# A new start for a gated SSM + GELU kernel: first tokens in 128-row pieces, weight strips on two hardware queues, third GELU stage moved up

## The chip, the cores and the metric

The kernel runs on one core of a Trainium2 chip. The metric is the device time of one execution in microseconds (us). A run of a single core has no second die beside it to compare with, so a run counts as fast unless it is more than 1.5% above the fastest run of the same kernel; only fast runs are compared. Each run also has a granted clock: the share of TensorE's full clock that the chip's throttle let through. The kernel before takes 217.74 us (median of three, 217.73 to 218.23).

## The reference

For 2048 tokens of width 640, a gate mixes a diagonal state-space model (SSM) with a GELU block:

```python
x = A_x                                                   # 1 x 2048 x 640, bfloat16
g = sigmoid((x * gate_w).sum(-1, keepdims=True))
# A: dt = exp(log_dt); Lam_bar = exp(dt * Lambda); B_bar = ((Lam_bar - 1) / Lambda)[:, None] * B
#    h_t = Lam_bar * h_(t-1) + x_t B_bar^T   (complex, 640 states, serial over the tokens)
#    a   = 2 * real(h C^T) + x * Dskip
# B: b   = gelu(x @ w1 + b1) @ w2 + b2      (640 -> 1728 -> 640)
return g * a + (1 - g) * b
```

## The kernel before

Tokens are processed in four chunks of 512. All products need the tokens turned, 128 features on the partitions (`xT`). TensorE (PE) then has four kinds of stage: `ff1` (the product with w1, GELU stage), `ssm` (the products with B), `fin_b` (the product with w2) and `fin_a` (the product with C). VectorE (DVE) makes the scan of the SSM, ScalarE (ACT) the evictions, which copy results out of a bank (the memory that PE writes). `colA` and `colB` hold small parameters turned into columns, and `hs` holds the scanned states that `fin_a` reads. Only the start and the order of stages are touched by the change. The start loads 256 tokens plainly and turns them on PE, lets a DMA transpose fetch the other 256, and loads the first 768 columns of w1 as five **strips** of 128 rows (192 KB each), all on the hardware queue that the SP engine issues to:

```python
load_xn(0, 0, H)                                          # 256 tokens, 320 KB, SP
nc.scalar.dma_start(out=prmA[...], ...)                   # 3 small parameter rows, ACT queue
for kd in range(KD):                                      # the five strips of w1
    nc.sync.dma_start(out=w1a[kd][:], in_=B_w1[kd * P:(kd + 1) * P, 0:cut1])
nc.sync.dma_start_transpose(out=xT[0][:, :, H * P:CH], in_=x2d[H * P:CH, :])
for kd in range(KD):
    nc.sync.dma_start(out=w1b[kd][:, 0:F - cut1], in_=B_w1[kd * P:(kd + 1) * P, cut1:F])
# ... (cut)
nc.sync.dma_start_transpose(out=BT_re[:], in_=A_B_re[:, :])
nc.sync.dma_start_transpose(out=BT_im[:], in_=A_B_im[:, :])
# ... (cut: six warm-up matmuls of 512 columns and one of 256 on a zeroed tile)
for kd in range(KD):
    for a in range(H):
        nc.tensor.transpose(pT[kd][:, a * P:(a + 1) * P], xn[0][:, a, kd * P:(kd + 1) * P], ident[:])
nc.tensor.transpose(pA[:, 0:3 * KS], prmA[:], ident[0:3 * KS, 0:3 * KS])
for kd in range(KD):                                      # copies of the turned tokens, DVE and ACT in turn
    # ... (cut)
nc.vector.tensor_copy(out=colA[:], in_=pA[:, 0:3 * KS])   # starts the chain of the decay parameters
nc.scalar.activation(out=dt16[:], in_=ldt_c, func=ACT.Exp)
# ... (cut: the rest of that chain, then)
for kd in range(KD):
    for kf in range(FA):
        ff1_mm(banks[kf], 0, kf, kd, 0, HT)               # strips, first 256 tokens
# ... (cut) the same for tokens 256 to 511, inside which, after kd == 2:
            nc.tensor.transpose(pA[:, P:P + NB], prmB[:], ident[0:NB, 0:NB])
            nc.vector.tensor_copy(out=colB[:], in_=pA[:, P:P + NB])
            for j in range(KD):                           # the "w1b copies": the gate's column into w1b
                nc.vector.tensor_copy(out=w1b[j][:, n1b - 1:n1b], in_=pA[:, P + j:P + j + 1])
# ... (cut) order of the stages:
fin_b(0); fin_a(0); load_xn(2); ssm(2); gel_tile(2); ff1(2); fin_b(1); gates(2); fin_a(1)   # ...
```

Of the kernel before, what the change touches and what calls it, by code (L numbers as in the profile page):

```python
# [10 lines left out]
ALU = mybir.AluOpType  # L11
# [5 lines left out]
P = 128  # L17
# [10 lines left out]
TPC = CH // P  # L28
HD = D // 2
# [9 lines left out]
def kernel(  # L39
# [32 lines left out]
    def bank(dtype=F32):  # L72
        return ps.tile([P, CH * 4 // (4 if dtype == F32 else 2)], dtype, name="bank")
# [8 lines left out]
    BT_re = const.tile([P, KD, D], BF16, name="BT_re")  # L82
    BT_im = const.tile([P, KD, D], BF16, name="BT_im")
# [5 lines left out]
    prmA = const.tile([3 * KS, P], BF16, name="prmA")  # L89
    NB = KS + KF - 1  # L90
    prmB = const.tile([NB, P], BF16, name="prmB")
# [9 lines left out]
    warm = work.tile([P, CH], BF16, name="v")  # L101
# [8 lines left out]

    H = TPC // 2

# [5 lines left out]

    load_xn(0, 0, H)
    nc.scalar.dma_start(out=prmA[0:KS, :], in_=A_log_dt.rearrange("(j p) -> j p", p=P))  # L120
    nc.scalar.dma_start(out=prmA[KS:2 * KS, :], in_=A_Lambda_im.rearrange("(j p) -> j p", p=P))
    nc.scalar.dma_start(out=prmA[2 * KS:3 * KS, :], in_=A_Lambda_re.rearrange("(j p) -> j p", p=P))
    for kd in range(KD):
        nc.sync.dma_start(out=w1a[kd][:], in_=B_w1[kd * P:(kd + 1) * P, 0:cut1])  # L124
    nc.sync.dma_start_transpose(out=xT[0][:, :, H * P:CH], in_=x2d[H * P:CH, :])  # L125
# [10 lines left out]
    nc.scalar.dma_start(out=prmB[KS:NB, :], in_=B_b1[0:(KF - 1) * P].rearrange("(j p) -> j p", p=P))  # L136
    nc.scalar.dma_start(out=prmB[0:KS, :], in_=gate_w.rearrange("(j p) -> j p", p=P))
    nc.sync.dma_start(out=b1x[:, 0:F_LAST], in_=B_b1[F - F_LAST:F].rearrange("(o d) -> o d", o=1).to_broadcast([P, F_LAST]))  # L138
    nc.sync.dma_start_transpose(out=BT_re[:], in_=A_B_re[:, :])  # L139
    nc.sync.dma_start_transpose(out=BT_im[:], in_=A_B_im[:, :])  # L140
# [15 lines left out]
    class Clock:  # L156
        pe = 5.0
        act = 13.0
# [5 lines left out]
    def later(ready, cost, fn):  # L164
        pend.append((ready, cost, fn))

    def let_out(until):
        while pend:
            ready, cost, fn = pend[0]
            start = max(ck.dve, ready)  # L170
            if start >= until:
                return
            pend.pop(0)
            fn()
            ck.dve = start + cost
# [14 lines left out]
    nc.vector.memset(warm[:], 0.0)  # L190
# [3 lines left out]
    wps = bank()  # L194
    for _ in range(6):
        nc.tensor.matmul(wps[:], lhsT=warm[:, 0:P], rhs=warm[:], start=True, stop=True)
    nc.tensor.matmul(wps[:, 0:2 * P], lhsT=warm[:, 0:P], rhs=warm[:, 0:2 * P], start=True, stop=True)
    pA = bank(BF16)
    pT = [bank(BF16) for _ in range(KD)]
    for kd in range(KD):  # L200
        for a in range(H):
            nc.tensor.transpose(pT[kd][:, a * P:(a + 1) * P], xn[0][:, a, kd * P:(kd + 1) * P], ident[:])
    HT = H * P
    nc.tensor.transpose(pA[:, 0:3 * KS], prmA[:], ident[0:3 * KS, 0:3 * KS])

    def col(name, dtype=F32, n=KS):
        return const.tile([P, n], dtype, name=name)
# [7 lines left out]
    for kd in range(KD):  # L215
        dst = xT[0][:, kd, 0:HT]
        if kd % 2 == 0:
            nc.vector.tensor_copy(out=dst, in_=pT[kd][:, 0:HT])
        else:
            nc.scalar.activation(out=dst, in_=pT[kd][:, 0:HT], func=ACT.Identity)  # L220
    nc.vector.tensor_copy(out=colA[:], in_=pA[:, 0:3 * KS])
    nc.scalar.activation(out=dt16[:], in_=ldt_c, func=ACT.Exp)
    nc.vector.tensor_copy(out=dt32[:], in_=dt16[:])
    nc.vector.tensor_tensor(out=dtl[:], in0=dt32[:], in1=lre_c, op=ALU.mult)
    nc.vector.tensor_tensor(out=th_c[:], in0=dt32[:], in1=lim_c, op=ALU.mult)
    nc.vector.tensor_scalar(out=thp_c[:], in0=th_c[:], scalar1=INV_2PI, scalar2=None, op0=ALU.mult)
    nc.scalar.activation(out=r_c[:], in_=dtl[:], func=ACT.Exp)


    scr = gelp.tile([P, KF * CH // 2], F32, name="gel")  # L230
    HB = 2 * HC

    def scratch(i):
        return scr[:, i * KS * HC:(i + 1) * KS * HC].rearrange("p (k i) -> p k i", k=KS)

    u, red, ab = scratch(0), scratch(1), scratch(2)
    m1, m2 = scratch(3), scratch(4)
    FSC = hsp.tile([P, 2 * KS, HB], F32, name="hs")
    FS = FSC[:, 0:KS, :]
    FC = FSC[:, KS:2 * KS, :]  # L240
    NQ = 4
    two = col("two", n=NQ * KS)
    kq = col("kq", I32, n=NQ * KS)
    redq = col("redq", n=NQ * KS)
    absq = col("absq", n=NQ * KS)
    sq = col("sq", n=NQ * KS)
    cq = col("cq", n=NQ * KS)
    kk = work.tile([P, KS, HC], I32, name="bu", bufs=8)

    def over(c):  # L250
        return c.rearrange("p (k o) -> p k o", o=1).to_broadcast([P, KS, HC])

    nc.vector.tensor_tensor(out=u, in0=tf[:].rearrange("p (o i) -> p o i", o=1).to_broadcast([P, KS, HC]), in1=over(thp_c[:]), op=ALU.mult)
    nc.vector.tensor_copy(out=kk[:], in_=u)
    nc.vector.tensor_tensor(out=red, in0=u, in1=kk[:], op=ALU.subtract)
    sth, cth = sq[:, 0:KS], cq[:, 0:KS]
    sL, cL = sq[:, KS:2 * KS], cq[:, KS:2 * KS]
    sH, cH = sq[:, 2 * KS:3 * KS], cq[:, 2 * KS:3 * KS]
    sQ, cQ = sq[:, 3 * KS:4 * KS], cq[:, 3 * KS:4 * KS]


# [3 lines left out]
    def ff1_mm(p, c, kf, kd, t0=0, t1=CH):  # L265
        w = w1a[kd][:, kf * P:(kf + 1) * P] if kf < FA else w1b[kd][:, (kf - FA) * P:(kf - FA + 1) * P]
        nc.tensor.matmul(p[:, t0:t1], lhsT=w, rhs=xT[c][:, kd, t0:t1], start=(kd == 0), stop=(kd == KD - 1))  # L267
        pe(t1 - t0)
# [33 lines left out]
    def ff1(c, k0=0):  # L302
        for kf in range(k0, KF - 1):
            p = bank()
            if kf == KF - 3:
                last = last_bank(c)
            for kd in range(KD):
                ff1_mm(p, c, kf, kd)
            ff1_act(p, c, kf)
            let_out(ck.pe)  # L310
        last_tile(c, *last)
        let_out(ck.pe)
# [4 lines left out]

    gel_tile(0)
    banks = [bank() for _ in range(FA)]
    for kd in range(KD):  # L320
        for kf in range(FA):
            ff1_mm(banks[kf], 0, kf, kd, 0, HT)
# [10 lines left out]
    for kd in range(KD):  # L333
        for kf in range(FA):
            ff1_mm(banks[kf], 0, kf, kd, HT, CH)
        if kd == 2:
            nc.tensor.transpose(pA[:, P:P + NB], prmB[:], ident[0:NB, 0:NB])
            nc.vector.tensor_copy(out=colB[:], in_=pA[:, P:P + NB])
            for j in range(KD):
                nc.vector.tensor_copy(out=w1b[j][:, n1b - 1:n1b], in_=pA[:, P + j:P + j + 1])  # L340
# [69 lines left out]
    def scan_ops(c, ks, bu, ready):  # L410
# [58 lines left out]
        later(0, 0.7, f8)  # L469

    def ssm(c):
        hs[c] = hsp.tile([P, 2 * KS, CH], BF16, name="hs")
        for ks in range(KS):
            bu = work.tile([P, 2, CH], BF16, name="bu", bufs=8)
            for ri, BT in enumerate((BT_re, BT_im)):
                p = bank()
                for kd in range(KD):
                    nc.tensor.matmul(p[:], lhsT=BT[:, kd, ks * P:(ks + 1) * P], rhs=xT[c][:, kd, :],  # L478
                                     start=(kd == 0), stop=(kd == KD - 1))
                    pe(CH)  # L480
                nc.scalar.activation(out=bu[:, ri, :], in_=p[:], func=ACT.Identity)  # L481
                act(0.6)
            scan_ops(c, ks, bu, ck.act)
            if c == 0 and ks == 0:
                later(0, 1.6, factors)
            let_out(ck.pe)
# [27 lines left out]
    def fin_b(c):  # L514
        for a in range(TPC):
            ti = c * TPC + a
            lo = a * P
            gb = fwork.tile([P, D], F32, name="gb")
            if a >= TPC - 2:
                seed(c * TPC + a - (TPC - 2))  # L520
            for d0, d1 in HALVES:
                p = bank()
                for kf in range(KF):
                    m = P if kf < KF - 1 else F_LAST + 1
                    nc.tensor.matmul(p[:, 0:d1 - d0], lhsT=gel[c][:m, kf, lo:lo + P], rhs=w2_sb[:m, kf, d0:d1],  # L525
                                     start=(kf == 0), stop=(kf == KF - 1))
                    pe(d1 - d0)
                nc.scalar.activation(out=gb[:, d0:d1], in_=p[:, 0:d1 - d0], func=ACT.Identity, scale=gcol[:, 1, ti:ti + 1])  # L528
                act(0.5)
            gbs[ti] = gb  # L530
            let_out(ck.pe)

    def fin_a(c):
        for a in range(TPC):
# [33 lines left out]
    fin_b(0)  # L568
    fin_a(0)
    load_xn(2)  # L570
    ssm(2)
    gel_tile(2)
    ff1(2)
    fin_b(1)
    gates(2)
# [41 lines left out]
```

## Time and profile before

| | before |
|---|---|
| median (first three runs) | 217.74 us |
| the profiled run | 218.23 us, span 216.2 us |
| first real matmul starts | 5.26 us |
| first SSM matmul starts | 21.13 us |
| PE's last matmul ends | 213.17 us |

The prediction below shows the busy times and the chain. Of four further views of the start, two stand here and two behind the prediction. The first is the timeline of what SP issued in the first 10 us: start, time in which these issues lay, queue, operation, tile and number.

```profile
1.25 3.47 SPq L124 DMA_DIRECT2D w1a<-in_B_w_dram  x5
4.77 2.04 SPq L125 DMA_TRANSPOSE xT<-in_A_x_dram  x1
6.86 2.47 SPq L127 DMA_DIRECT2D w1b<-in_B_w_dram  x5
```

The strips are issued first, then the transpose, then w1b: one queue, in this order. The second is the list of DMA issues in 3 to 13 us; its last column is the median time from issue to landing.

```profile
xT<-in_A_x_dram SPq DMA_TRANSPOSE x1, 4.3
```

The third is ACT's timeline. The bracket in a timeline gives the idle time ahead and what ended it.

```profile
2.66 1.28 ACT L220 ACT_TABLE_LOAD   x1 [2.66 <-issue]
```

The load of the activation tables takes 1.28 us, but it is done at 3.94, and ACT then still waits for PE's first transposes until 4.60: the load costs nothing here.

### The profile page before, as it was taken

The numbers are of one execution on the slowest core, as the hardware profiler recorded it, in microseconds if no ns is written. First come the engines' busy times: TensorE is split into PE (matmuls) and PEld (weight loads), VectorE is DVE, ScalarE is ACT, GpSimd is POOL, SyncE is SP. The second block draws the span as 40 slices with busy tenths as digits, with TensorE's granted clock in tenths as the row PEclk, the third lists the DMA queues.
The fourth block names the chain that finished last, engine by engine and source line by source line (L and its number), as shares of the span: only waits on it lengthen the run. The fifth ranks groups of instructions, "written<-read, shape, count | busy, mean of one in ns | idle before, by whom it ended". The sixth has DMA issues, their size and how long they took to land.

```text
span 216.2 us, 3470 instructions
## 1 busy us (share of the span) xinstructions
PE 211.9 (98%) x1368; PEld 128.2 (59%) x1368; DVE 189.8 (88%) x393; ACT 91.7 (42%) x156; POOL 1.6 (1%) x12
## 2 busy tenths in 40 slices
PE   7999999999999999999999999999999999999994
PEld 3855444454577775444477777444457777777773
DVE  3889999999999899999999999999999999961152
ACT  3689456675696101556642200456662210022100
POOL 2000000000000000000000000000000000000000
PEclk9999999999999999999999999999999999999999
DMA  5999999995000042000010006100001000100011
GB/s 174 255 224 199 226 214 369 175 246 103 3 0 0 0 141 106 0 0 3 0 24 3 0 0 200 45 2 0 0 3 24 0 3 30 61 30 3 2 61 61
DMA packets 32339, 16.16 MB, mean 75 GB/s; under 512 B 25091, under 2 KB 32324, under 8 KB 32324
## 3 DMA queue, kind: packets, MB, share of 16 engines
q1 hardware_dynamic: 32114, 15.91, 30.2%
q8 instruction: 10, 0.16, 0.3%
q10 hardware_dynamic: 210, 0.04, 0.1%
q14 instruction: 5, 0.04, 0.1%
HBM read 7.24 MB, written 2.62 MB: 46 GB/s over the span
## 4 chain that ended last, share of the span: by engine, by line
PE 88%; SPq 5%; DMA 5%; issue 0%; DVE 0%
PE bank L525 28%; PE bank L544 20%; PE bank L478 20%; PE bank L267 19%; DMA BT_im<-in_A_B_im_dram 3%; SPq L139 3%; DMA xn<-in_A_x_dram 1%; SPq L127 1%; SPq L125 1%; PE bank L292 1%; SPq L124 0%; SPq L138 0%; DVE ot L549 0%
## 5 line engine op out<-in xcount | busy, mean ns | idle before, releaser
L525 PE MATMUL bank<-w_sb,gel 128*128 128x320 bf16 x448 | 61.6, 299 | 0.0
L525 PEld LDWEIGHTS <-gel 128*128 128x128 bf16 x448 | 43.6, 98 | 17.2
L481 ACT ACTIVATE bu<-bank 128x512 bf16<-128x512 f32 x40 | 23.9, 597 | 41.7 <-PE bank L478 41.7
L271 ACT ACTIVATE gel<-bank,colB 128x512 bf16<-128x512 f32 x52 | 34.6, 693 | 15.1 <-PE bank L267 14.8
L544 PEld LDWEIGHTS <-hs 128*128 128x128 bf16 x330 | 31.8, 98 | 11.9
L434 DVE TENSOR_TENSOR_SCAN g<-r_c,carry,v 128x512 bf16<-128x512 f32 x30 | 37.2, 1270 | 0.0
L528 ACT ACTIVATE gb<-bank,gcol 128x320 f32<-128x320 f32 x32 | 16.5, 527 | 48.2 <-PE bank L525 46.6
L267 PE MATMUL bank<-xT,w1b 128*128 128x512 bf16 x140 | 31.0, 379 | 0.0
L267 PE MATMUL bank<-xT,w1a 128*128 128x512 bf16 (+1 forms) x150 | 27.6, 344 | 0.0
L544 PE MATMUL bank<-CT_im,hs 128*128 128x320 bf16 (+2 forms) x165 | 27.1, 295 | 0.0
L544 PE MATMUL bank<-CT_re,hs 128*128 128x320 bf16 (+2 forms) x165 | 27.1, 295 | 0.0
L549 DVE SCALAR_TENSOR_TENSOR ot<-bank,gcol,gb 128x320 bf16<-128x320 f32 (+2 forms) x33 | 17.3, 533 | 9.5 <-PE bank L544 9.3
L478 PE MATMUL bank<-xT,BT_im 128*128 128x512 bf16 x100 | 24.9, 379 | 0.1
L478 PE MATMUL bank<-xT,BT_re 128*128 128x512 bf16 x100 | 24.8, 379 | 0.0
L267 PEld LDWEIGHTS <-w1b 128*128 128x128 bf16 x140 | 13.6, 98 | 16.3 <-DMA w1b<-in_B_w_dram 0.3
L267 PEld LDWEIGHTS <-w1a 128*128 128x128 bf16 x150 | 14.9, 100 | 11.7
L511 DVE TENSOR_TENSOR bank<-xn,Dbc 128x320 f32<-128x320 bf16 (+2 forms) x33 | 14.3, 483 | 5.8 <-ACT gb L528 5.8
L478 PEld LDWEIGHTS <-BT_im 128*128 128x128 bf16 x100 | 9.7, 98 | 12.2 <-DMA BT_im<-in_A_B_im_dram 0.6
L478 PEld LDWEIGHTS <-BT_re 128*128 128x128 bf16 x100 | 9.7, 98 | 11.0
L415 DVE TENSOR_TENSOR v<-wa,wb 128x512 bf16<-128x512 bf16 x40 | 15.2, 421 | 0.7
L415 DVE TENSOR_TENSOR wa<-TCOS,g 128x1024 bf16<-128x1024 bf16 x20 | 13.7, 686 | 0.1
L415 DVE TENSOR_TENSOR wb<-TSIN,g 128x1024 bf16<-128x1024 bf16 x20 | 13.7, 684 | 0.0
(98 smaller groups left out, 130.7 us busy)
## 6 DMA issues: line engine op xcount, KB each, us to landing
out_dram<-ot SPq DMA_DIRECT2D x15, 160.0 KB, 1.8
w_sb<-in_B_w_dram SPq DMA_DIRECT2D x1, 2080.0 KB
xn<-in_A_x_dram SPq DMA_DIRECT2D x3, 640.0 KB, 4.9
w1b<-in_B_w_dram SPq DMA_DIRECT2D x5, 240.0 KB, 4.2
w1a<-in_B_w_dram SPq DMA_DIRECT2D x5, 192.0 KB, 3.5
xn<-in_A_x_dram SPq DMA_DIRECT2D x2, 320.0 KB
Dbc<-in_A_Dskip_dram SPq DMA_DIRECT2D x1, 160.0 KB
out_dram<-ot SPq DMA_DIRECT2D x1, 128.0 KB
```

What stands on the lines that cost most here:

```text
L139: nc.sync.dma_start_transpose(out=BT_re[:], in_=A_B_re[:, :])
L267: nc.tensor.matmul(p[:, t0:t1], lhsT=w, rhs=xT[c][:, kd, t0:t1], start=(kd == 0), stop=(kd == KD - 1))
L271: nc.scalar.activation(out=gel[c][:, kf, :], in_=p[:, :], func=ACT.Gelu_apprx_tanh, bias=b1_c[:, kf:kf + 1])
L415: nc.vector.tensor_tensor(out=o, in0=a, in1=b, op=op)
L434: nc.vector.tensor_tensor_scan(s["g"][:, ri, :], r_c[:, ks:ks + 1].to_broadcast([P, CH]), s["v"][:, ri, :], init, ALU.mult, ALU.add)
L478: nc.tensor.matmul(p[:], lhsT=BT[:, kd, ks * P:(ks + 1) * P], rhs=xT[c][:, kd, :], start=(kd == 0), stop=(kd == KD - 1))
L481: nc.scalar.activation(out=bu[:, ri, :], in_=p[:], func=ACT.Identity)
L511: dve_now(ck.pe, 0.45, lambda: nc.vector.tensor_tensor(out=p[:, 0:d1 - d0], in0=xn[c][:, a, d0:d1], in1=Dbc[:, d0:d1], op=ALU.mult))
L525: nc.tensor.matmul(p[:, 0:d1 - d0], lhsT=gel[c][:m, kf, lo:lo + P], rhs=w2_sb[:m, kf, d0:d1], start=(kf == 0), stop=(kf == KF - 1))
L528: nc.scalar.activation(out=gb[:, d0:d1], in_=p[:, 0:d1 - d0], func=ACT.Identity, scale=gcol[:, 1, ti:ti + 1])
L544: nc.tensor.matmul(p[:, 0:d1 - d0], lhsT=hs[c][:, j, lo:lo + P], rhs=CT[:, j % KS, d0:d1], start=False, stop=(j == 2 * KS - 1), skip_group ...
L549: nc.vector.scalar_tensor_tensor(out=ot[:, d0:d1], in0=p[:, 0:d1 - d0], scalar=gcol[:, 0, ti:ti + 1], in1=gbs[ti][:, d0:d1], op0=ALU.mult, ...
```

## The change

The intent is to start real work earlier. The first 128 tokens come in a load of their own and are turned by plain matmuls against the identity. Strips 0, 2 and 4 go to ACT's hardware queue, 1 and 3 to SP's, ahead of the DMA transpose. `colA` is taken later, after strip 2. B comes in two parts, and the third GELU stage moves in front of `fin_a(0)`. The core of the diff, with cuts:

```diff
-    load_xn(0, 0, H)
-    nc.scalar.dma_start(out=prmA[0:KS, :], ...)            # three rows
-    for kd in range(KD):
-        nc.sync.dma_start(out=w1a[kd][:], in_=B_w1[kd * P:(kd + 1) * P, 0:cut1])
-    nc.sync.dma_start_transpose(out=xT[0][:, :, H * P:CH], in_=x2d[H * P:CH, :])
+    load_xn(0, 0, 1)
+    load_w1a(nc.scalar, 0)
+    load_xn(0, 1, H)
+    # ... memsets of prmA, prmB
+    rows(nc.scalar, prmA[0:KS, :], A_log_dt)               # three rows
+    load_w1a(nc.sync, 1)
+    load_w1a(nc.scalar, 2)
+    load_w1a(nc.sync, 3)
+    load_w1a(nc.scalar, 4)
+    rows(nc.scalar, prmB[KS:NB, :], B_b1[0:(KF - 1) * P])
+    rows(nc.scalar, prmB[0:KS, :], gate_w)
+    nc.sync.dma_start_transpose(out=xT[0][:, :, HT:CH], in_=x2d[HT:CH, :])
 ...
-    nc.sync.dma_start_transpose(out=BT_re[:], in_=A_B_re[:, :])
-    nc.sync.dma_start_transpose(out=BT_im[:], in_=A_B_im[:, :])
+    for r0, r1, part in ((0, KSA * P, 0), (KSA * P, KS * P, 1)):
+        nc.sync.dma_start_transpose(out=BT_re[part][:], in_=A_B_re[r0:r1, :])
+        nc.sync.dma_start_transpose(out=BT_im[part][:], in_=A_B_im[r0:r1, :])
 ...
+    # warm-up on a constant: 6 matmuls of 512 columns, 2 of 128
+    def turn(p, col, a, kd):
+        nc.tensor.matmul(p[:, col:col + P], lhsT=xn[0][:, a, kd * P:(kd + 1) * P], rhs=ident[:], ...)
+    # ... five turns of tokens 0 to 127, copied by DVE in pieces
+    strip(0, 0, P, True)
+    # ... five turns of tokens 128 to 255, copied by DVE (2) and ACT (2 copies, 3 turns)
+    strip(1, 0, P, False)
+    strip(0, P, HT, False)
+    strip(1, P, HT, False)
+    strip(2, 0, HT, False)
+    nc.tensor.matmul(pA[:, P:P + 3 * KS], lhsT=prmA[:], rhs=ident[:, 0:3 * KS], ...)
+    nc.vector.tensor_copy(out=colA[:], in_=pA[:, P:P + 3 * KS])
+    # ... the chain of decay parameters
+    for kd in range(3, KD):
+        strip(kd, 0, HT, False)
 ...
     fin_b(0)
+    gel_tile(2)
+    ff1(2, 0, (0, 1))
+    gates(2)
     fin_a(0)
     load_xn(2)
     ssm(2)
-    gel_tile(2)
-    ff1(2)
     fin_b(1)
-    gates(2)
```

## The prediction

> **What bounds the kernel now.** I read the page's first part (busy time by engine), then the chain of waits in order of time, then the head with the timeline of one engine at a time.
>
> ```profile
> PE 211.9 (98%) x1368; PEld 128.2 (59%) x1368; DVE 189.8 (88%) x393; ACT 91.7 (42%) x156; POOL 1.6 (1%) x12
> ...
> 15.48 0.04 issue
> 15.52 6.92 DMA BT_im<-in_A_B_im_dram
> 22.45 0.05 issue
> 22.49 9.89 PE bank L478 x45
> 32.38 14.03 PE bank L267 x65
> ...
> 57.81 15.25 PE bank L525 x112
> 73.06 10.87 PE bank L544 x80
> ```
>
> Chain columns: start, duration, what. From 22.49 to the last output at 213.2 us the chain is matmuls without a gap: 190.7 us. Its pieces run at the array's pace: 65 matmuls of 512 columns in 14.03 us are 216 ns each. No matmul of this stretch is removed, so only the 22.49 us ahead of it can shrink. There, three losses are visible.
>
> ```profile
> L267 PE MATMUL bank<-xT,w1a 128*128 128x256 bf16 x8 | 1.9, 413 | 0.0
> L267 PE MATMUL bank<-xT,w1a 128*128 128x256 bf16 x53 | 6.2, 275 | 0.0
> PEld L478 <- DMA BT_im<-in_A_B_im_dram: 0.6, 1, 0.6
> SPq L124 <- DMA xn<-in_A_x_dram: 1.3, 1, 1.3
> ```
>
> The first line is PE's groups by shape in 3.9 to 6.9 us, the second the same in 7.0 to 12.8; the others are waits (total, times, longest), the last one the SP queue's own. (1) The same matmul takes 413 ns early and 275 later. Eight started in the 1.64 us from 5.26 to 6.9, 205 ns apiece, where 256 columns later cost 109: 8 x 0.096 = **0.8 us** lost. (2) Five BT_re matmuls end about 21.13 + 5 x 0.216 = 22.21; the next starts at 22.49: **0.28 us** lost (the 0.6 is the weight load's wait, which runs ahead). (3) Real work starts only at 5.26, after a 320 KB load landed at 3.90 and ten transposes. Nothing else is lost: 35 matmuls and one of 260 columns fill 12.84 to 20.51 (35 x 0.216 + 0.11 = 7.66 of 7.67).
>
> Two things sit right behind PE there.
>
> ```profile
> 5.45 0.16 DVE L221 CAST colA<-bank 128x15 f32<-128x15 bf16 x1
> ...
> 10.40 0.18 DVE L330 SCALAR_TENSOR_TENSOR absq<-redq 128x20 f32<-128x20 f32 x1
> 11.63 0.18 DVE L338 CAST colB<-bank 128x18 f32<-128x18 bf16 x1 [1.05 <-PE bank L337]
> 11.72 0.41 DVE L340 COPY w1b<-bank 128x1 bf16<-128x1 bf16 x5
> ...
> 71.79 0.42 DVE L415 TENSOR_TENSOR hs<-wb,wa 128x512 bf16<-128x512 bf16 x1
> ```
>
> In the DVE timeline, colA starts a DVE chain (decay parameters, table arguments) that ends at 10.58, 5.13 us later with 0.28 idle; colB and the five w1b copies come after it in DVE's order and finish at 12.13. And the last hs of chunk 0 ends at 72.21, while PE begins to use it at 73.06: under 1 us of slack. A PE that only got faster would wait there.
>
> **What the Trainium skill says.** "TensorE: Matmul & The Clock Gate", Part 1: the array runs at half clock until one window of about 3.4 us has been busy. The trace agrees on the ratio (205 against 109 ns per matmul). The release at about 6.9 us is 5.7 us after the first warm-up matmul at 1.18. Part 4 of that page says that transpose-mode matmuls do not count as busy for this; no run so far shows that, but it would explain plain matmuls in place of transposes. The same page's "Back-to-back issue gap" gives N/2.4 + 2.5 ns: 216 for 512, agreeing; 56 for 128, and half clock doubles the first term. "DMA: Bandwidth & Descriptors", Rules for kernel authors, says that two issuing queues share the same 16 engines and save only issue time. The trace has 0.43 us of SP time per strip, and a DMA busy share around 0.9 from 2 us on, so I expect earlier issue, not more bandwidth.
>
> **The change, part by part.**
>
> *Start.* Warm-up no longer waits for a memset: about 0.85 instead of 1.18. Six of 512 and two of 128 cold columns (427 and 107 ns) take 2.8 us, ending near 3.6. The first 160 KB of x shares its way with one 192 KB strip; the old 320 KB landed at 3.90, so I put it at 3.4. A turn (0.3 latency) and a small DVE copy (0.2 to 0.25, from 0.29 for 256 columns) give first real work at about 4.2: 1.05 us earlier.
>
> *Work of PE.* Columns are equal: 24 matmuls of 128 and 48 of 256 for 60 of 256; twelve more x 2.5 ns is 0.03 us. Five turns now fall after the start: 0.3 us warm, 0.5 cold. Left to itself, PE would leave this stage up to 1 us earlier, more if the clock comes early.
>
> *DMA.* SP issues two of the five strips instead of all: the transpose and the w1b loads move up about 1 us. The first strips need not wait for 320 KB of x. Total bytes before w1b's end are the same, so I allow 0.5 to 0.9 us for the w1b landings, needed until 14.56 before.
>
> *The DVE chain is later.* colA is now taken after strip 2, the third weight strip. Strip 2 needs 0.9 MB landed (about 5.3 us by my estimate) and all matmuls before it. If the clock is released by about 4.2, strip 2 ends near 6.0 and colA starts at 6.2; released at 5.5: 7.25; at 6.95 as now: 8.0. Adding 5.13 + 0.2 (colB) + 0.45 (copies) gives 12.0, 13.05 or 13.8 for the end of the copies. The eight banks are six strips, one turn bank and pA; the next two matmul groups (two_banks) need both of the latter, and pA is free only after those copies. Today PE arrives at 12.84, the copies being done at 12.13. After, PE would be there at 11.4 to 12.5, and **waits for DVE**. Net at this point: +0.8, -0.2 or -1.0 us.
>
> *BT in two parts.* The first 256 rows of both land before PE asks: +0.28 us.
>
> *Third GELU stage moved up.* It puts 14.6 us between fin_b(0) and fin_a(0). No wait for hs existed at 73.06, so it gains nothing itself; it is the insurance for an earlier PE. Its cost is later ssm(2), but DVE starts scan(2) only at 111.74 (scans of chunk 1 from 72.9) and the new ssm(2) runs about 98 to 109, so DVE does not starve. At the end DVE finishes hs of chunk 3 at 191.2 against PE's need at 202.3: 11 us of slack, enough for a DVE that starts its tables up to 1.7 us later. I book 0.
>
> Sum: gain 1.1, 0.1 or -0.7 us for early, middle or late clock. I weigh these 0.45, 0.4, 0.15 because plain matmuls and an earlier warm-up should bring the clock earlier: 0.50 + 0.04 - 0.10 = 0.43, about **0.5 us**. 217.74 - 0.5 = 217.2.
>
> **Rivals.** *A: the head is worth its full 1.5 to 2 us* (1.05 start, 0.8 clock, 0.28 BT). For it: all three losses are real, and the chain behind is solid PE. Against it: colA's chain and w1b landings, both close already. It would give 215.8 to 216.2. *B: DVE's chain takes over entirely* with a late clock: 218.4. For it: 5.13 us without a gap; against it: strip 2 may come early. *C: the reorder stalls PE in mid-kernel*, through seeds issued late by a lagging DVE or banks held by four seeds during the third GELU stage. Against it: seeds of tiles 0 and 1 are issued over 3 us before use and three banks stay for rotation, with an eviction of 0.69 us per 1.08 us of matmul. If it did: 1 to 3 us, up to 220. *D: the reorder frees DVE stalls I do not see.* PE has no gaps to give, so nothing.
>
> **Range and chances.** Early clock with a quick colA gives 216.1, late clock with a little stall 218.4: the range is 216.1 to 218.4. Faster by 2% needs 213.4, 4.3 us less; all head losses together are about 2.2, so 0.02. Slower by 2% needs 4.4 us of new stalls: only C could, 0.03.
>
> **What would show it.** In the changed profile: first L267-type matmul at about 4.2; short matmuls at twice their warm pace until the clock is released, and when that is; colA start at 6.2 to 8.0; a PE gap before the first w1b matmuls that ends with the w1b copies; no BT_im wait; no PE idle from about 22 us on; fin_a(0) near 87. Wrong if: colA comes before 6, PE does not wait for the copies, or a matmul gap appears after 25 us.

## More of the kernel before

The fourth is PE's timeline at the first real matmuls:

```profile
5.26 6.22 PE L267 MATMUL bank<-xT,w1a 128*128 128x256 bf16 x48
```

## The result and the profile after

The changed kernel takes 221.26 us (median of four, 219.51 to 222.42) beside 217.74 (217.46 to 218.23) before. The ratio is 1.015 (95% interval 1.010 to 1.020). Recorded mean clocks are 0.992 (the profiled run), 0.999, 0.998 and 0.998. A ratio here is the mean time of one kernel's fast runs over that of the other's of the same rounds, so it is not quite the ratio of the medians. The prediction was 217.2 with a range of 216.1 to 218.4, so the measured time lies 2.9 us above the range. The profiled run is the slowest of the four (222.42), and that of before is the slowest of its own (218.23).

Ordered as before, first the busy times of the page, then the chain in order of time (start, duration, what):

```profile
PE 212.8 (96%) x1370; PEld 129.6 (59%) x1381; DVE 189.2 (86%) x396; ACT 91.5 (41%) x156; POOL 1.6 (1%) x12
```

```profile
0.73 2.97 DMA w1a<-in_B_w_dram
...
3.72 0.37 ACTq L119
...
4.13 7.62 DMA w1a<-in_B_w_dram
11.75 0.05 issue
11.79 4.04 PE bank L246 x24
...
26.13 10.52 PE bank L519 x48
...
91.97 3.12 PE bank L586 x23
```

PE's busy time grew by 0.9 us, far less than the 4.4 us by which the span grew. The chain now starts with two weight strips. It reads: strip 0 landed at 3.70, **which let ACT's queue issue the next strip** at 3.72; the last strip was issued at 4.13 and landed 7.62 us later, at 11.75; that let PE go on at 11.79. The chain of before had its last DMA at 22.45 and was PE alone after it; here PE is alone from 11.79 on, and `fin_a(0)` starts at 91.97 without a gap ahead of it. The loss is in the head. PE's timeline there:

```profile
4.24 0.80 PE L246 MATMUL bank<-xT,w1a 128*128 128x128 bf16 x6
...
7.80 0.82 PE L246 MATMUL bank<-xT,w1a 128*128 128x256 bf16 x6 [0.80 <-ACT xT L220]
...
11.79 4.04 PE L246 MATMUL bank<-xT,w1a 128*128 128x256 bf16 x24 [2.50 <-DMA w1a<-in_B_w_dram]
15.63 0.22 PE L378 MATMUL bank<-ident,prmB 128*128 128x18 bf16 x1
...
17.42 5.56 PE L246 MATMUL bank<-xT,w1b 128*128 128x512 bf16 x24
```

Real work does start at 4.24 instead of 5.26. Then PE stands for 0.80 us for a copy by ACT and for 2.50 us for strip 4. After that it runs slowly: 24 matmuls of 256 columns take 3.84 us (11.79 to 15.63), 160 ns each, where the free pace is 109. I read a ledger from this. "Ideal" is what PE's matmuls of the stretch take at the full clock (after: 24 x 0.056 + 48 x 0.109 + five turns, 0.28 + two parameter turns, 0.06 + 7.66 for the w1b part + 0.61 for the 20 narrow matmuls behind it; before, 60 of 256 columns at 0.109 in place of the first three terms, and one parameter turn, 0.03).

| from the first real matmul to the first SSM matmul | before | after |
|---|---|---|
| starts, ends | 5.26, 21.13 | 4.24, 25.86 |
| length | 15.87 | 21.62 |
| ideal | 14.85 | 15.19 |
| lost at half clock, first time | 0.8 | 1.0 |
| waits: ACT's copy; strip 4 | 0 | 0.80; 2.50 |
| lost at half clock, second time (13.15 to 16.57) | 0 | 1.7 |
| rest | 0.2 | 0.4 |

The first SSM matmul comes 4.73 us later: 1.02 us gained at the start, 0.34 lost to narrower work, 5.41 more lost to waits and clock. PE's end moves from 213.17 to 217.44, 4.27 us. The difference of 0.46 holds the wait for BT_im, 0.28 before, which is gone.

Why was strip 4 so late? The issues of SP (first two lines) and ACT:

```profile
3.54 2.22 SPq L138 DMA_TRANSPOSE xT<-in_A_x_dram  x1
5.81 6.83 SPq L140 DMA_DIRECT2D w1b<-in_B_w_dram  x5
```

```profile
0.73 0.41 ACTq L119 DMA_DIRECT2D w1a<-in_B_w_dram  x1
2.10 0.31 ACTq L122 DMA_DIRECT2D prmA<-in_A_Lambda_re_dram  x1
3.72 0.85 ACTq L119 DMA_DIRECT2D w1a<-in_B_w_dram  x2
...
6.07 1.28 ACT L220 ACT_TABLE_LOAD   x1 [6.07 <-DVE xT L218]
7.36 0.55 ACT L220 ACTIVATE xT<-bank 128x256 bf16<-128x256 f32 x2
```

ACT was done with the rows at 2.41 and issued nothing until 3.72. As the trace's instructions show, strip 2's issue waits for the semaphore that counts the landing of strip 0, and strip 4's for that of the second token piece: only eight completion semaphores serve all these loads, and each later load waits for the one that last used its semaphore. So strips 2 and 4 went out *after* the transpose on the other queue, and moved beside it. The landing times, from the list of DMA issues in 3 to 13 us:

```profile
xT<-in_A_x_dram SPq DMA_TRANSPOSE x1, 8.8
w1a<-in_B_w_dram ACTq DMA_DIRECT2D x2, 192.0 KB, 5.8
```

The transpose needs 8.8 us instead of 4.3, the two strips 5.8 in the median instead of 3.5 for the five of before. The same timeline shows a second thing: ACT's table load begins at 6.07, not at 2.66, because in ACT's order it now stands behind ACT's wait for DVE's copies; so ACT's copies of the tokens come after 7.36, and PE waits. Behind that wait, DVE's `colA` starts at 8.68:

```profile
8.68 0.17 DVE L322 COPY colA<-bank 128x15 f32<-128x15 f32 x1 [2.69 <-PE bank L321]
...
13.64 0.18 DVE L371 SCALAR_TENSOR_TENSOR absq<-redq 128x20 f32<-128x20 f32 x1
...
16.00 0.41 DVE L381 CAST w1b<-bank 128x1 bf16<-128x1 f32 x5
```

The chain takes 5.14 us, as before, and the w1b copies end at 16.41. PE was so late itself that it did not wait for them: it came to w1b at 17.42.

Last, slices of 1 us: length, busy time of PE, PEld, DVE, ACT and POOL with counts, granted clock, DMA share, GB/s. First before:

```profile
10.00:11.00 1.00, 1.00 (x12) 0.89 (x10) 0.51 (x3) 0.93 (x3) 0.00 (x0) 1.00 1.07 355
```

and after:

```profile
10.00:11.00 1.00, 0.00 (x0) 0.00 (x0) 0.97 (x2) 1.00 (x1) 0.00 (x0) 1.00 1.10 147
13.00:14.00 1.00, 1.00 (x8) 0.72 (x6) 0.72 (x6) 1.00 (x3) 0.00 (x0) 0.58 0.88 273
```

In the slice from 10 us the DMA engines count as equally busy (1.1) and move less than half as much (147 for 355 GB/s). And the granted clock falls to 0.58 after the idle stretch. (The column says 1.00 before the first record of a throttle, so the cold start must be read from the durations of matmuls or from the start of that record.) By the mean clocks above, the profiled run is the only one of the four that was throttled a second time.

### The profile page after: what moved, and what is told of

Read it like the earlier page. It is cut to its first block, busy times and chain, and to the rows that moved or that the text cites. A ratio compares the mean times of both kernels' runs of the same rounds, so it can differ in the third digit from the quotient of the medians.

```text
span 220.6 us, 3495 instructions
## 1 busy us (share of the span) xinstructions
PE 212.8 (96%) x1370; PEld 129.6 (59%) x1381; DVE 189.2 (86%) x396; ACT 91.5 (41%) x156; POOL 1.6 (1%) x12
## 4 chain that ended last, share of the span: by engine, by line
PE 93%; DMA 5%; issue 0%; ACTq 0%; DVE 0%
PE bank L566 28%; PE bank L246 25%; PE bank L586 20%; PE bank L519 19%; DMA w1a<-in_B_w_dram 5%; PE bank L272 1%; ACTq L119 0%; DVE ot L591 0%; PE bank L262 0%; PE bank L378 0%
## 5 line engine op out<-in xcount | busy, mean ns | idle before, releaser
L246 PE MATMUL bank<-xT,w1a 128*128 128x512 bf16 (+2 forms) x159 | 29.4, 345 | 3.5 <-DMA w1a<-in_B_w_dram 2.5
L246 PEld LDWEIGHTS <-w1a 128*128 128x128 bf16 x162 | 16.1, 107 | 15.7 <-DMA w1a<-in_B_w_dram 3.7
L456 DVE TENSOR_TENSOR wa<-TCOS,bu 128x1024 bf16<-128x1024 bf16 x20 | 13.7, 683 | 0.0
```

Source lines behind the costliest of these rows:

```text
L246: nc.tensor.matmul(p[:, t0:t1], lhsT=w, rhs=xT[c][:, kd, t0:t1], start=(kd == 0) if first is None else first, stop=(kd == KD - 1), skip_gr ...
L456: nc.vector.tensor_tensor(out=o, in0=a, in1=b, op=op)
```

## The experiments

My theories after this reading. The **strip theory** (A, later narrowed to A2): strips on ACT's queue land late. In its first form the second queue itself does it; narrowed, it is that they are issued late, behind earlier landings, and then move beside the transpose. The **chain theory**: colA, delayed by ACT's table load and by its new place, makes PE wait for the w1b copies, hidden in this run by the strip. **Rivals**: the moved stage costs something; or PE's idleness is dear only through the throttled clock. Runs of before: medians 217.63 (7 runs), 217.86 (11) and 217.66 (11). All outputs were correct. Each expectation uses its own short letters.

### s1_strips_sp: the changed kernel, all strips on SP

```diff
-    load_w1a(nc.scalar, 0)      # and 2 and 4
+    load_w1a(nc.sync, 0)        # and 2 and 4
```

> The changed kernel with all five weight strips issued from the SP queue ahead of the DMA transpose, the rest as changed. Theory A (strips 2 and 4, issued from the ACT queue after 3.7 us, move side by side with the DMA transpose and both crawl): strip 4 lands near 7 instead of 11.75 us, PE's 2.5 us wait for it is gone, the transpose lands near 9 as before; time 217 to 218. Rival R (the moved third stage costs the time) and rival T (the small pieces and the later decay chain cost it): no gain over the changed kernel, 220 to 222, the wait replaced by one of about the same size.

Measured: 219.23 us (218.82 to 219.28), ratio 1.0071 (1.0056 to 1.0086). No strip is waited for. PE's timeline shows what is left:

```profile
7.71 0.81 PE L246 MATMUL bank<-xT,w1a 128*128 128x256 bf16 x6 [1.00 <-ACT xT L220]
...
13.00 0.38 PE L246 MATMUL bank<-xT,w1b 128*128 128x512 bf16 x1
14.21 5.35 PE L246 MATMUL bank<-xT,w1b 128*128 128x512 bf16 x24 [0.84 <-DVE w1b L381]
```

About half of the loss is gone, less than expected. PE now arrives at 13.00, can do one matmul, and waits for DVE's w1b copies: this is the wait that the prediction described, and it appears as soon as the strips no longer hide it.

### s2_before_two_queues: the kernel before, strips 2 and 4 on ACT's queue

```diff
-        nc.sync.dma_start(out=w1a[kd][:], in_=B_w1[kd * P:(kd + 1) * P, 0:cut1])
+        (nc.scalar if kd in (2, 4) else nc.sync).dma_start(out=w1a[kd][:], in_=B_w1[kd * P:(kd + 1) * P, 0:cut1])
```

> The kernel before with only strips 2 and 4 moved to the ACT queue. Theory A: strip 4 is again issued beside the transpose and lands late (9 to 12 us), PE waits 1 to 4 us for it, time 219 to 222. Rivals R and T: this part is harmless, 217.5 to 218.

Measured: 217.74 us (217.48 to 217.89), ratio 1.0006 (0.9991 to 1.0021). A second queue alone costs nothing that shows (0.2% at most), so the first form of the strip theory fell. Here ACT issued both strips from 1.98 to 2.82, with no wait for a landing ahead, and SP issued the transpose at 4.11; no strip was waited for. (PE did wait 0.9 us for ACT's token copies, because the strip issues pushed the table load to 4.73.) What differs from the changed kernel is *when* the strips are issued.

### s3_stage_back: the changed kernel, third GELU stage back in its old place

```diff
-            if a >= TPC - 2 and c > 0:
+            if a >= TPC - 2:
 ...
     fin_b(0)
-    gel_tile(2)
-    ff1(2, 0, (0, 1))
-    gates(2)
     fin_a(0)
     load_xn(2)
     ssm(2)
+    gel_tile(2)
+    ff1(2)
     fin_b(1)
+    gates(2)
```

> The changed kernel with the third GELU stage put back where it was. Theory A: the head keeps its loss; because DVE is then late for the hs of chunk 0 by about as much as PE, at most 1 us more: 220.5 to 222.5. Rival R: back to 217 to 218.

Measured: 220.57 us (220.0 to 221.12), ratio 1.0137 (1.0111 to 1.0162). The interval overlaps that of the changed kernel. The head's waits are there as before (2.8 us for strips, 0.6 for ACT's copy), and there is no new one. The moved stage is not the cause.

### s4_pe_busy: the changed kernel, ten dummy matmuls ahead of strip 4

```diff
     for kd in range(3, KD):
+        if kd == KD - 1:
+            for _ in range(10):
+                nc.tensor.matmul(pA[:], lhsT=ones(P), rhs=ones(512), start=True, stop=True)
         strip(kd, 0, HT, False)
```

> The changed kernel with ten dummy matmuls of 512 columns (2.2 us) between strip 3 and strip 4, in PE's wait. Theory A with the clock as second cost: strip 4 lands as late as before (11.5 to 12 us), but the array is not throttled again at about 13 us; runs that were throttled lose up to 1.7 us less, so 219.3 to 220.5 with a smaller spread. If the re-throttling were no part of it: 221 to 222, as the changed kernel.

Measured: 220.73 us (220.11 to 221.25), ratio 1.0136 (1.0107 to 1.0165). In its profile the clock was full from 6.31 on and not throttled again, yet strip 2 was waited for 1.5 us. By the recorded mean clocks (0.999 and more) none of its four runs was throttled again, and of the changed kernel's four only the profiled one was. A cost of 1.7 us in one run of four would be an estimated 0.4 us on average. The gain at the medians is about 0.5 us, which fits, but it is within the spread of both kernels. A kept clock does not give the loss back.

### e5_rows_late: the changed kernel, parameter rows issued after the strips

```diff
     load_xn(0, 1, H)
-    rows(nc.scalar, prmA[0:KS, :], A_log_dt)                 # and the two others
     load_w1a(nc.sync, 1)
     load_w1a(nc.scalar, 2)
     load_w1a(nc.sync, 3)
     load_w1a(nc.scalar, 4)
+    rows(nc.scalar, prmA[0:KS, :], A_log_dt)                 # and the two others
```

> The changed kernel with the five small parameter rows issued after the weight strips on the ACT queue. Strips 2 and 4 then need no semaphore that an earlier load must free, and are issued by about 2 us, well before the DMA transpose (3.5 us). Theory A2 (not the second queue itself but strips that move while the DMA transpose moves): strip 4 lands at 6 to 7.5 us, the transpose by 8 to 9, no PE wait for a strip over 0.5 us; time 218 to 219.5, what is left being the late decay chain and table load as with all strips on SP. Rival A1 (any strip on the second queue is slowed next to SP traffic): strip 4 after 9 us, 220 to 222.

Measured: 220.39 us (219.7 to 221.44), ratio 1.0125 (1.0099 to 1.0151). The DMA half of the expectation held: strip 4 was issued at 1.66, not 4.13, and landed at 7.05, and the transpose needed 5.1 us, not 8.8. The time missed the expectation. Strip 1 now landed late (PE waited 1.0 us), the rows came so late that colA's matmul ran at 10.38, and the clock of the profiled run stayed at half until 13.12. The edit moved two things at once and can't price either.

### e6_before_beside: the kernel before, strips 2 and 4 forced to move beside the transpose

The strips' issue on ACT's queue has to wait for the tokens, through one copied element that the load then overwrites:

```diff
     # ... (cut: two parameter rows of prmB are issued earlier on ACT's queue, around these loads)
+    for kd in (0, 1, 3):                                      # these stay on SP
+    for kd in (2, 4):
+        nc.vector.tensor_copy(out=w1a[kd][:, 0:1], in_=xn[0][:, 0, 0:1])
+        nc.scalar.dma_start(out=w1a[kd][:], in_=B_w1[kd * P:(kd + 1) * P, 0:cut1])
```

> The kernel before with strips 2 and 4 on the ACT queue and made to wait (by one copied element) until x has landed, about 4 us, so that they move beside the DMA transpose. A2: strip 4 takes over 6 us from issue to landing and the transpose over 6.5 us (4.3 before); PE waits 1 to 3 us for a strip; time 219.5 to 222, part of it from the table load behind the later DMA issues (up to 1 us). If the overlap were harmless: strip 4 lands by 8.5 us, transpose by 9, at most 1 us slower than before.

Measured: 218.86, 219.72 and 219.88 us (a fourth run, 222.82, counts as slow and is left out), ratio 1.0079 (1.0057 to 1.0102). The mean clock of the run left out is 0.992, as in the profiled run of the changed kernel, so it may have been throttled again rather than disturbed from outside; with it the ratio of the means would be about 1.011. From its waits of PE (total, times, longest):

```profile
PE bank L270 <- DMA w1a<-in_B_w_dram: 1.0, 1, 1.0
PE bank L270 <- ACT xT L223: 0.9, 1, 0.9
```

The old kernel shows the new one's waits when its strips are issued late on the other queue. It is milder than expected: strip 4 needed 5.3 us from issue to landing and the transpose 6.3. The second line shows that this edit, too, delays ACT's table load, so not all of the 0.8% is the strips'; s2 had that wait as well and lost nothing.

### e7_sp_early: strips on SP, and the table load and colA early

This is s1 with a one-column activation ahead of everything on ACT (so that the tables are loaded while ACT has nothing to do), and with colA taken right after the first five turns:

```diff
+    tbl = const.tile([P, 1], F32, name="tbl")
+    nc.scalar.activation(out=tbl[:], in_=halfpi[:], func=ACT.Exp)
 ...
+    nc.tensor.matmul(pA[:, 2 * P:2 * P + 3 * KS], lhsT=prmA[:], rhs=ident[:, 0:3 * KS], ...)
+    nc.vector.tensor_copy(out=colA[:], in_=pA[:, 2 * P:2 * P + 3 * KS])
 ...
     strip(2, 0, HT, False)
-    nc.tensor.matmul(pA[:, P:P + 3 * KS], lhsT=prmA[:], rhs=ident[:, 0:3 * KS], ...)
-    nc.vector.tensor_copy(out=colA[:], in_=pA[:, P:P + 3 * KS])
```

> The changed kernel with all strips on SP, one tiny activation ahead so that the table is loaded early, and the decay columns (colA) taken right after the first five turns. Theory C (what is left in the SP-only variant is the DVE chain from colA and the table load): colA starts at about 5 instead of 8.6 us, the copies into w1b end by 12, PE does not wait for them; time 216.5 to 217.5, so 0 to 0.5% faster than before. If theory C is wrong: 218.5 to 219.5 as the SP-only variant.

Measured, five rounds: 217.53 us (217.36 to 218.13), ratio 0.9992 (0.9979 to 1.0006). PE's timeline:

```profile
5.69 5.39 PE L250 MATMUL bank<-xT,w1a 128*128 128x128 bf16 x54 [0.56 <-DMA w1a<-in_B_w_dram]
...
12.26 5.61 PE L250 MATMUL bank<-xT,w1b 128*128 128x512 bf16 x25
```

No wait for copies is left; the 25 matmuls of w1b run on. The whole loss is given back with these two repairs. Nothing is won over the kernel before, though.

### e8_gp_early: e5 with the early chain, rows on GpSimd's queue

```diff
-    rows(nc.scalar, prmA[0:KS, :], A_log_dt)                 # and the other rows
+    rows(nc.gpsimd, prmA[0:KS, :], A_log_dt)                 # and the other rows
+    # table load and colA early, as in e7
```

> As the previous one, but strips on both queues as the change has them and the parameter rows on GpSimd's queue, so that no strip waits for a semaphore and the transpose is issued at about 2.7 us. A2: strips land by 7 and the transpose by 8, about 1 us earlier than before; time 216.0 to 217.2. If strips and transpose still collide (the transpose may catch up with strips in flight): a PE wait over 1 us for a strip, 218 or more.

Measured: 221.97 us (220.9 to 222.98), ratio 1.0196 (1.0167 to 1.0224). The expectation missed, and one line of PE's waits says why:

```profile
PE bank L232 <- DMA prmA<-in_A_Lambda_re_dram: 2.8, 1, 2.8
```

From GpSimd's queue the rows needed 4.7 to 5.3 us each and the last landed at 7.8. PE stood for them at the early colA, though strip 0 had landed at 3.55. This run was a bad design; it says nothing on the strips.

### x1_early_two_queues: the changed kernel with the early chain only

It is the fourth corner of a square: the strips stay on two queues, and the table load and colA come early as in e7.

```diff
-    load_w1a(nc.sync, 0)      # of e7; and 2 and 4
+    load_w1a(nc.scalar, 0)    # and 2 and 4
```

> The changed kernel as it is (strips on both queues) with only the early table load and the early colA. If the two costs are hidden one behind the other (PE waits for strip 4 until 11.8 us, the DVE chain ends before PE is back), this gains little: 220 to 221.5, PE's wait for strip 4 only longer by what strip 2 no longer waits. If the chain is a cost of its own next to the strip wait: 219 to 219.8, as much better as it was with all strips on SP (1.7 us).

Measured: 219.55 us (218.66 to 220.45), ratio 1.0087 (1.0055 to 1.0119). The only wait of PE that its profile lists is not for a strip:

```profile
PE bank L232 <- DMA prmA<-in_A_Lambda_re_dram: 0.7, 1, 0.7
```

The early colA waits for the parameter rows, whose first packets moved at 3.09, behind strip 0 on ACT's queue (2.35 in e7). Real work starts at 5.26 (4.18 in e7), and half clock lasts until 9.22 (3.66 in e7). Strip 4 landed at 10.31, and PE, slow until then, began with it at 10.36. ACT's table load came at 5.56, behind the strips' issues, hardly earlier than the 6.07 of the changed kernel. So this corner pays for the two queues in another way than the changed kernel does, and the square prices the arrangement of the queues as a whole, not the wait for strip 4 alone. The four corners, as ratios to before:

| | strips on two queues | strips on SP | cost of the two queues |
|---|---|---|---|
| chain late | 1.0150 (changed kernel) | 1.0071 (s1) | 0.79% |
| chain early | 1.0087 (x1) | 0.9992 (e7) | 0.95% |
| cost of the late chain | 0.63% | 0.79% | |

Each difference is uncertain by 0.2 to 0.6 points, and within that the costs add. At 217.7 us the strips' place on two queues costs 1.7 to 2.1 us and the late chain with the table load 1.4 to 1.7.

### x2_all_turned: e7 without the DMA transpose at the start

```diff
-    nc.sync.dma_start_transpose(out=xT[0][:, :, HT:CH], in_=x2d[HT:CH, :])
+    load_xn(0, H, TPC)
 ...
-    for kd in range(3, KD):
+    for kd, a in ((3, 2), (4, 3)):
+        # five more turns of tokens a * 128 on, copied by ACT
         strip(kd, 0, HT, False)
```

> A version meant to beat both: the SP-only variant with early colA and table, and no DMA transpose at the start at all: the second 256 rows of x are loaded plainly (a load that the kernel made later anyway) and turned by ten more plain matmuls, copied by ACT. If the DMA transpose is what slows the start (4.3 us from issue to landing, next to strips and w1b): no PE wait over 0.5 us after 4.2 us, first SSM matmul at 20.0 to 20.6 (21.13 before), time 216.2 to 217.0, 0.3 to 0.7% faster than before. If PE's own work is the limit: 217 to 217.6, as without it.

Measured, five rounds: 219.56 us (219.07 to 219.97), ratio 1.0082 (1.0064 to 1.0100). It was an attempt at a better version, and it missed. The plain load was issued at 4.95 and landed at 9.3, and PE waited 0.9 us for it. It also waited 0.6 us for the additional copies by ACT, which pushed ACT's next table load to 11.6 and its first sine to 12.9.

### x3_before_bt: the kernel before with B in two parts

```diff
-    nc.sync.dma_start_transpose(out=BT_re[:], in_=A_B_re[:, :])
-    nc.sync.dma_start_transpose(out=BT_im[:], in_=A_B_im[:, :])
+    for r0, r1, part in ((0, KSA * P, 0), (KSA * P, KS * P, 1)):
+        nc.sync.dma_start_transpose(out=BT_re[part][:], in_=A_B_re[r0:r1, :])
+        nc.sync.dma_start_transpose(out=BT_im[part][:], in_=A_B_im[r0:r1, :])
```

> The kernel before with only BT loaded in two parts. My prediction booked 0.28 us for it: no PE wait for BT_im, 217.3 to 217.6, a ratio of 0.9987 or so; if it were worth nothing 217.6 to 217.9.

Measured, five rounds: 217.73 us (217.53 to 218.05), ratio 1.0000 (0.9984 to 1.0016). The wait for BT_im is gone from the profile. Its 0.28 us would be 0.13%, which is inside the interval: neither shown nor excluded.

### x5_e7_stage_back: e7 with the third GELU stage back

The edit is that of s3, made to e7.

> The SP-only variant with early colA and table, with the third GELU stage put back. As insurance theory has it: PE now comes to the SSM output of chunk 0 about 0.8 us earlier than before and DVE about as late as before, so PE waits there 0.3 to 1.0 us: 217.8 to 218.5. If DVE keeps ahead: same as with the stage moved, 217.4 to 217.6.

Measured, five rounds: 217.76 us (217.67 to 219.76), ratio 1.0016 (0.9987 to 1.0045), which overlaps e7's. PE has no wait at `fin_a(0)` in the profile. So even with the head repaired, the insurance of the moved stage wasn't drawn on.

### The strip and the transpose, packet by packet

The traces also hold each DMA packet. Strip 4 has 128 packets of 1536 bytes and the transpose 1280 of 256. This is the time from the first to the last packet of each, in eight profiled runs, and the rate of all DMA traffic from the first to the last packet of both:

| | strip 4 (us) | transpose (us) | both, first to last | all DMA in that time (GB/s) |
|---|---|---|---|---|
| before (one queue) | 1.2 | 2.3 | 2.4 | 232 |
| s1 (one queue) | 1.3 | 2.1 | 2.4 | 242 |
| e7 (one queue) | 1.3 | 2.1 | 2.4 | 234 |
| s2 (two queues, strip first) | 1.9 | 2.7 | 3.3 | 258 |
| e5 (two queues, strip first) | 2.4 | 2.6 | 3.8 | 246 |
| e6 (two queues, transpose first) | 2.1 | 3.2 | 3.7 | 201 |
| x1 (two queues, transpose first) | 3.9 | 3.9 | 4.2 | 184 |
| after (two queues, transpose first) | 4.7 | 4.9 | 5.4 | 143 |

On one queue the two follow each other and are through in 2.4 us. On two queues their packets mix, and the two need up to 5.4 us: twice as long in all, and nearly four times as long for the strip. Part of this is that other loads (w1b, strips) move in the longer time as well, so the last column is the fairer measure. With the strip first the rate is that of one queue, and nothing is lost. With the transpose first it falls, to 143 GB/s in the changed kernel (160 and 141 in s3 and s4, which have its head), while the engines count as equally busy (1.1 to 1.2 throughout). Why this mix is slower is not settled by these runs.

## Why the prediction was wrong

**Start: right.** The first real matmul was put at 4.2 and came at 4.24. Turning 128 tokens by plain matmuls does what it is meant to.

**Work of PE: right.** The stretch's ideal grew by 0.34 us, as booked (0.03, and 0.3 to 0.5 for five turns).

**DMA: the step that failed.** It read "SP issues two of the five strips instead of all: the transpose and the w1b loads move up about 1 us", and took from it a gain. The transpose's issue did move up, from 4.77 to 3.54. I worked out one queue's issue times and not the other's: strips 2 and 4, on ACT's queue, had to wait for earlier landings and went out at 3.72 and after, later than the transpose that they were to precede. The wait that did it stands in the prediction's own lines: "SPq L124 <- DMA xn" is the old kernel's queue standing 1.3 us for an earlier landing, and the prediction did not ask where such waits would fall after the change. "Earlier issue, not more bandwidth" left out that the two could take bandwidth from each other: both slowed (table above), strip 4 landed at 11.75, and SP's w1b loads did not gain either (issued from 5.81, but over 6.83 us rather than 2.47). Measured in the place of a gain: a cost of 1.7 to 2.1 us (s1 against the changed kernel, e7 against x1). Only the first pair shows the wait for strip 4 as its main part (2.50 us, and 2.43 in s3 with the same head); in x1 the same placing cost its time through late rows and a late clock. e6 brings a wait of 1.0 us for a strip into the old kernel. No run takes away the late issue alone and wins the time back: e5 took it away, but its late rows and late clock came in its place. So the price of the two queues is shown, and how much of it is strip 4's wait is in part argued.

**The DVE chain: right mechanism, wrong size.** I put colA between 6.2 and 8.0, the end of the copies at 12.0 to 13.8, and a PE wait there. The term that was missed is ACT's table load: 1.28 us, free at 2.66 before, at 6.07 in the path after, because its place in ACT's order had moved behind a wait. With it, colA came at 8.68. In the changed kernel PE was later still, so the wait did not show (by the prediction's own sign, "PE does not wait for the copies", it was wrong there); s1 laid it bare (0.84 us), and the square prices chain and table load together at 1.4 to 1.7 us. The prediction had this stage at +0.8, -0.2 or -1.0.

**The clock: the weights had no ground.** "Plain matmuls and an earlier warm-up should bring the clock earlier" was my reason for 0.45 on an early clock. By the clock records of the traces, the release from half clock came, in the profiled runs, at 3.86, 4.92, 5.28 and 6.95 us in kernels with transposes (s2, e6, x3 and before) and at 3.66, 3.92, 4.15, 4.25, 5.21, 6.31, 6.33, 9.22, 11.76 and 13.12 in those with plain matmuls. Neither kind is earlier. So the 0.8 us that the prediction took as a loss of the kernel before belonged to one execution: x3, with the same start, was released at 5.28 and lost nothing.

In these records every stretch but a run's last lasts a whole multiple of 3.413 us (in the profile after 6.83 at full clock, then 3.41 at half, then 204.80 at full). The times therefore fit a window of 3.41 us that runs freely: the array is released at the end of one in which PE was busy enough. As the profile counts busy time, the windows that released it were 78% (s2) to 100% busy; windows of 76 to 79% in x1, e5 and e8 did not release it. Where the window lies differs from one execution to the next, and a start with waits in it may miss one or two. It also fits the second throttling in the profile after: the window from 9.74 to 13.15 was some 40% busy, and half clock followed for 3.42 us. But in s3 a window that was 42% busy (7.33 to 10.74) was not followed by half clock, so the limit is not known. I take the spread of the changed kernel, 2.9 us where before has 0.8, to come from the clock. For its slowest run the mean clock of 0.992 shows it; for the rest it is argued, not shown, since only one execution of each kernel has a profile.

**BT in two parts: not resolved.** The wait is gone, and its worth of 0.28 us lies within the interval of x3.

**Stage moved up: right.** I booked 0; s3 and x5 agree, within about 0.5%. PE had no gap past 26 us, and rival C, the only one that I let reach 220, did not happen. The time went beyond it through the head, which none of the rivals had at that size.

The sum by the square: two queues 1.7 to 2.1 us, chain and table load 1.4 to 1.7, everything else in the change together (e7 against before) between 0.5 us less and 0.1 us more. These are steps of one path from before to the changed kernel, so they add up to its loss, 3.3 us by the ratio and 3.5 by the medians, by construction. In this last entry one thing stays open: e7 starts 1 us earlier than before and yet is not faster. Its profile shows 0.56 us of waiting for strip 1 and 0.34 of extra PE work, which takes most of it. x3's profile, with the old start and the clock released at 5.28, comes to its first SSM matmul at 20.69, e7's at 20.59. What else the runs without a profile lose is not known.

## What to carry to other kernels

When loads are moved to a second queue, write down for *each* queue when every load is issued, what earlier landing that issue waits for, and what will be moving at that time; a load that is meant to precede a DMA transpose and ends up beside it can take several times as long (here 4.7 us of packets where it had 1.2). When an instruction is moved back in an engine's order, look for what hides behind it, such as a table load that was free only because it happened early. And a loss that is found first can hide a second one of the same size, so undo suspects one at a time *and* together, as the square of four runs did.

## What the Trainium skill lacked or had wrong

- "DMA: Bandwidth & Descriptors", Rules for kernel authors, says that spreading DMAs over issuing queues doesn't help bandwidth and that a transpose next to ordinary DMAs needs nothing. The second holds for correct results (all runs were correct), but for time a warning is missing: around a 192 KB strip and a 320 KB transpose all DMA moved 232 to 242 GB/s with both on one queue, and 143 to 201 with the strip on a second queue behind the transpose, at a busy share of 1.1 to 1.2 in both cases. So a second queue can lose bandwidth; with the strip ahead (246 and 258 GB/s) it did not. The same page's advice of a dedicated semaphore per DMA doesn't give the price of sharing: here a strip's issue stood from 2.41 to 3.72 us for an earlier landing.
- "TensorE: Matmul & The Clock Gate", Part 4, says that transposes don't count as busy for the clock. The traces speak against it: before was released at 6.95 after a window (3.54 to 6.95) of which ten transposes held more than a third. Without them that window was 67% busy, as was the one in x3, while windows of plain matmuls busy at 76 to 79% (x1, e5, e8) did not release the clock. And the releases with transposes (3.86 to 6.95) aren't later than those with plain matmuls (3.66 to 13.12). Part 1 of the page, that the window of about 3.4 us is free-running and that the number of cold matmuls varies from run to run, agrees with the runs; but throttling again needed no idle window, as a wait of 2.50 us (a window some 40% busy) sufficed once, and one of 2.43 us in s3 (42% busy) did not.
